# Lightning attention from the second group on in sub-chunks of 64: four products as 64x64 quarters

## The chip, the cores and the metric

The kernel runs on one core of a Trainium2 chip. TensorE multiplies (PE, with its weight loads as PEld), VectorE (DVE) and ScalarE (ACT) do the elementwise work, GpSimd (POOL) and SyncE (SP) mostly issue transfers. The metric is device time in microseconds (us) of one execution; the median of three runs of the kernel before is 673.94 us (673.93 to 674.11). A change of less than 0.2% can't be told from none.

## The reference

Inputs are q, k and v (4 batches, 8 heads, 768 positions, 64 dimensions), a decay per head, lam, and two weight matrices. First comes causal attention without a softmax, with a running state, in blocks of 64 positions:

```python
for b in range(nb):
    qb, kb, vb = (q[:, :, sl], k[:, :, sl], v[:, :, sl])
    intra = np.einsum('bhic,bhjc->bhij', qb, kb) * Dmask[None]      # lam ** (i - j), i >= j
    intra = np.einsum('bhij,bhjd->bhid', intra, vb)
    inter = np.einsum('bhid,bhde->bhie', qb * lam_pow[None], kv_state)
    out[:, :, sl] = intra + inter
    kb_dec = kb * rev_pow[None]
    kv_state = lam_block[None, :, None, None] * kv_state + np.einsum('bhsd,bhse->bhde', kb_dec, vb)
```

Its output, seen as x of 3072 tokens x 512, then goes through `h = x @ w_in` (512 x 2048), `g = h - tanh(h)` and `g @ w_out` (2048 x 512). The block length is free in exact arithmetic: any block length gives the same output.

## The kernel before, in words

The 768 positions are cut into six groups of 128 (`BLK`, `NG`); one group over four batches is 512 tokens. For each group the kernel does the attention, then the up product with w_in, the tanh step, and the down product with w_out. The two big products go by Strassen's scheme: seven products of sums of blocks in place of eight, and from the second group on some of the seven are split once more in the same way (`down_twice`, with the small products' results in the banks y and zw). The sums of blocks are made by VectorE: `sums_once`, `sums_twice`, and inside `down_twice` the step that subtracts s2 from a12, which the sixth of its seven products (x = 3) reads.

The attention of group g + 1 is computed in pieces between the up and down products of group g, a half (two batches) at a time. Its functions are these. `att_transpose` makes transposed q and k; from group 2 on VectorE transposes 32x32 blocks of specially loaded tiles (L306), and then makes qd, q times the powers of lam (L317). `att_scores` multiplies k and q (L327: 64 rows, 128 columns of weights, 128 moving columns, for each head) into the banks sp, and VectorE multiplies with the mask of decays (L331). `att_out` adds two products in the banks op: the inner product of state and qd (L375: 64x64 quarters, 128 columns) and the intra product of v and the masked scores (L381: 128 rows, 64 columns of weights, 128 columns). ScalarE copies the result to xt (L385). `att_state` multiplies k by its decay (L336), makes the product of k and v over the 128 positions (L349: 128 rows, 64 columns of weights, 64 moving columns) and updates the state (L354, L355). `att_sums` (L392 to L395) makes the Strassen sums of x once both halves are there.

Six places in the schedule take the attention of the next group: two in the last two steps of the up product (u = 2 and 3), one after each of the down products 2, 4, 5 and 6. Before, they take in this order: transposes of the first half; its scores; its output and state; transposes of the second half; its scores; its output, state and the sums. Group 1's attention is spread in the same six portions over group 0's plain down product. The order of instructions on each engine is not the program's alone: a scheduler moves whatever is not marked `keep_in_program_order` (`tied` in the code). Matrix banks in PSUM for the attention are four, shared in turn (tag "att").

A matmul of the program in float32 is two weight loads and two matmul records in the profile.

Of the kernel before, what the change touches and what calls it, by code (L numbers as in the profile page):

```python
# [9 lines left out]
F32 = mybir.dt.float32  # L10
# [3 lines left out]
AF = mybir.ActivationFunctionType  # L14
AL = mybir.AluOpType

BLK = 128
GB = 2
GRP = 512
CLAMP = 2.0 ** -15  # L20
# [3 lines left out]
def kernel(  # L24
# [32 lines left out]
    nc = tc.nc  # L57
    B, H, S, D = q.shape
    NTOK, DM = out.shape
    DFF = moe_w_in.shape[1]  # L60
    NP = H // 2
# [36 lines left out]
            nc.vector.tensor_tensor_scan(out=mask[:, j, p, :], data0=lam_all[:, h:h + 1].to_broadcast([128, BLK]),  # L98
                                         data1=ident, initial=0.0, op0=AL.mult, op1=AL.add)

    fwd = const.tile([128, NP, BLK], F32)

    def powers():
        for j in range(2):
            tc.keep_in_program_order(nc.vector.tensor_copy(
                fwd[ts(j, 64), :, 0], lam_all.rearrange("s (p j) -> s j p", j=2)[ts(j, 64), j, :]))
        m = 1
        while m < BLK:
            tc.keep_in_program_order(nc.vector.tensor_tensor(
                fwd[:, :, m:2 * m], fwd[:, :, 0:m], fwd[:, :, m - 1:m].to_broadcast([128, NP, m]), op=AL.mult))  # L110
            m *= 2
# [1 line left out]

    bwd = mask.rearrange("s j p i -> s p j i")[:, :, :, BLK - 1:BLK].to_broadcast([128, NP, 2, D])

    lam_blk = fwd[:, :, BLK - 1:BLK][:, None, :, :].to_broadcast([128, 2, NP, D])

    def tied(yes, op):
        return tc.keep_in_program_order(op) if yes else op
# [6 lines left out]
    def load_natural(g, b, names):  # L126
        for name, src, bufs in (("q", q, 2), ("k", k, 3), ("v", v, 4)):
            if name in names:
                x = (qpool if name == "q" else io).tile([128, H, D], F32, name=f"{name}_nat", tag=name, bufs=bufs)
                op = nc.sync.dma_start(out=x, in_=src[b, :, ts(g, BLK), :].rearrange("h s d -> s h d"))  # L130
                tc.keep_in_program_order(op)
                raw[g, b][name] = x

# [11 lines left out]
    def load(n):  # L145

        while at["loaded"] < min(n, len(chunks)):
            g, b = chunks[at["loaded"]]  # L150
            if g < GB:
                raw[g, b] = {}
                load_natural(g, b, "qkv")
                at["loaded"] += 1
                continue
            for b in range(B):
                raw[g, b] = {}
            nat = "kv" if g < NG - 1 else "v"

            first = (0, 1, 2) if g == GB else ()  # L160
            for b in first:
                load_natural(g, b, nat)
            for b in range(B - 1):
                load_blocks(g, b, "qk")
            load_blocks(g, 3, "q")
            for b in (0, 1):
                if b not in first:
                    load_natural(g, b, nat)
            load_blocks(g, 3, "k")
            for b in (2, 3):  # L170
                if b not in first:
                    load_natural(g, b, nat)
            at["loaded"] += B
# [99 lines left out]
    def bank(name, tag, bufs):  # L273
        return psum.tile([128, 512], F32, name=name, tag=tag, bufs=bufs)
# [23 lines left out]
    def att_transpose(g, bs):  # L298
        for b in bs:
            load(g * B + b + 1)  # L300
            t = raw[g, b]
            qt = work.tile([128, NP, BLK], F32, name="qt", tag="qt")
            kt = work.tile([128, NP, BLK], F32, name="kt", tag="kt")
            for dst, x in ((qt, "q"), (kt, "k")):
                if g >= GB:
                    tc.keep_in_program_order(nc.vector.transpose(out=dst.rearrange("d p i -> d (p i)"),  # L306
                                                                 in_=t[x + "b"].rearrange("d p r a -> d (p r a)")))
                else:
                    tp = bank("tp", "att", 4).rearrange("d (p s) -> d p s", p=NP)
                    for p in range(NP):  # L310
                        tied(g == 0 or p == 0, nc.tensor.transpose(out=tp[:, p, :], in_=t[x][:, 2 * p:2 * p + 2, :],
                                                                   identity=ident))
                    tied(g == 0, nc.scalar.activation(dst, tp, AF.Copy))
            qd = None
            if g > 0:
                qd = work.tile([128, NP, BLK], F32, name="qd", tag="qd")
                nc.vector.tensor_tensor(qd, qt, fwd, op=AL.mult)  # L317
            tr[g, b] = (qt, kt, qd)

    def att_scores(g, bs):  # L320
# [12 lines left out]

    def att_decay(g, b):
        kp = raw[g, b]["k"].rearrange("s (p j) d -> s p j d", j=2)
        tied(g != 1, nc.vector.tensor_tensor(kp, kp, bwd, op=AL.mult))  # L336

    def att_state(g, bs):
        if g == NG - 1:
            return  # L340

        kv = bank("kv", "att", 4).rearrange("d (b p e) -> d b p e", b=2, p=NP)
        for n, b in enumerate(bs):
            kd, vn = raw[g, b]["k"], raw[g, b]["v"]
            if g > 0:
                att_decay(g, b)
            for p in range(NP):
                for j in range(2):
                    tied(g == 0, nc.tensor.matmul(out=kv[ts(j, 64), n, p, :], lhsT=kd[:, 2 * p + j, :],  # L349
                                                  rhs=vn[:, 2 * p + j, :], start=n == 0 and p == 0, stop=True,  # L350
                                                  skip_group_check=True))
        st = state[:, bs[0]:bs[0] + 2]
        if g > 0:
            nc.vector.tensor_tensor(st, st, lam_blk, op=AL.mult)  # L354
            nc.vector.tensor_tensor(st, st, kv, op=AL.add)  # L355
        else:
            tied(True, nc.scalar.activation(st, kv, AF.Copy))

    def att_out(g, bs):
        half = bs[0] // 2  # L360
        xt[g, half] = xpool.tile([128, KI, HB], F32, name=f"xt{half}", tag=f"xt{half}")

        ops = [bank("op", "att", 4).rearrange("d (p b s) -> d p b s", p=2, b=2) for _ in range(2)]

        def dst(n, p, j):
            return ops[p // 2][ts(j if p < 2 else 1 - j, 64), p % 2, n, :]


        if g > 0:
            for n, b in enumerate(bs):  # L370
                for p in (0, 1):
                    for j in range(2):
                        r = ts(j, 64)
                        for pp in (p, p + 2):
                            nc.tensor.matmul(out=dst(n, pp, j), lhsT=state[r, b, pp, :], rhs=tr[g, b][2][r, pp, :],  # L375
                                             start=n == 0 and p == 0, stop=False, skip_group_check=True)
        for n, b in enumerate(bs):
            ss, vn = sc.pop((g, b)), raw[g, b]["v"]
            for p in range(NP):
                for j in range(2):  # L380
                    tied(g == 0, nc.tensor.matmul(out=dst(n, p, j), lhsT=vn[:, 2 * p + j, :], rhs=ss[:, j, p, :],  # L381
                                                  start=g == 0 and n == 0 and p % 2 == 0,
                                                  stop=n == 1 and p % 2 == 1, skip_group_check=True))
        for x in range(2):
            tied(g == 0, nc.scalar.activation(  # L385
                xt[g, half][:, 2 * x:2 * x + 2, :].rearrange("d p (b s) -> d p b s", b=2), ops[x], AF.Copy))

    def att_sums(g, bs):
        x0, x1 = xt[g, 0], xt[g, 1]
# [6 lines left out]
        xt[g] = dict(B11=b11, B21=b21, B22=b22, T1=tt[:, 0], T2=tt[:, 1], T3=b12, T4=tt[:, 2])  # L396

    def attention(g):
        pieces = [[(fn, g, bs) for fn in (att_transpose, att_scores, att_out, att_state)] for bs in ((0, 1), (2, 3))]
        pieces[1].append((att_sums, g, None))  # L400
        return pieces


    FACT = {1: ("A11", "B11"), 2: ("A12", "B21"), 3: ("S4", "B22"), 4: ("A22", "T4"), 5: ("S1", "T1"),
# [374 lines left out]
    def run(pieces):  # L779
        for fn, *args in pieces:  # L780
            fn(*args)
# [33 lines left out]
    for u in range(1, NU):  # L815
# [4 lines left out]
            load(2 * B)  # L820
        if u == 1:
            powers()
    p0, p1 = attention(1)
    weights(len(blocks) - 2 * (KH - 2))
    more = [p0[0:1], p0[1:2], p0[2:], p1[0:1], p1[1:2], p1[2:]]
    for kt in range(KH):
        down_plain(kt)
        sums_out(kt)
# [15 lines left out]
    up(1, 0, 1)  # L844
    for g in range(1, NG):
        last = g == NG - 1
        p0, p1 = attention(g + 1) if not last else ([], [])
        for u in range(NU):
            for n in (2, 6, 5, 7, 1, 4, 3) if g < GI else (1, 7, 3) if u == 0 else (6, 5, 1, 7, 3) if u + 1 < NU else (
                    6, 5, 7, 1, 3):  # L850
# [16 lines left out]
            if g == GI - 1:  # L867
                inner_weights(u)
            if not last and u > 1:
                run(p0[u - 2:u - 1])  # L870
        if twice(g, 4):
            sums_twice(g, 4)
        every(down(g, 2))
        run(p0[2:])
        sums_twice(g, 5)
        every(down_twice(g, 4, "z") if twice(g, 4) else down(g, 4))
        run(p1[0:1])
        sums_once(g, 21, 21, 11)
        sums_twice(g, 6)
        every(down_twice(g, 5, "w"))  # L880
        run(p1[1:2])
        if twice(g, 7):
            sums_twice(g, 7)
        every(down_twice(g, 6, "z"))
        if twice(g, 3):
            sums_twice(g, 3)
        run(p1[2:])
        every(down_twice(g, 7, "w") if twice(g, 7) else down(g, 7))
        if last:
            down_end(g)  # L890
# [45 lines left out]
```

## Time and profile before

| what | value |
|---|---|
| median of three runs | 673.94 us |
| span of the profiled execution, first to last instruction | 672.3 us |
| that execution's granted TensorE clock | 1.000 throughout |
| TensorE matmul busy | 661.7 us, 4824 records |
| VectorE busy | 481.3 us, 872 instructions |
| ScalarE busy | 194.8 us |
| GpSimd busy | 200.5 us |
| scores, L327 | 384 records, 25.2 us busy |
| intra product, L381 | 384 records, 23.6 us busy |
| state product, L349 | 320 records, 11.5 us busy |
| inner product, L375 | 320 records, 11.0 us busy |

The span lies 1.6 us below the median: the time also has what lies around the first and the last instruction. "Busy" of a group is the time in which at least one of its instructions ran; since matmuls overlap, the mean length of one record is far above the distance between their starts. What a product costs TensorE is read from the timeline, from its first start to the first start of what follows.

### The profile page before, as it was taken

Reading aid. Unit: us, or ns where it says so; the run is one execution under the profiler, and the core shown is the slowest. Engines: PE = TensorE matmul, PEld = TensorE weight load, DVE = VectorE, ACT = ScalarE, POOL = GpSimd, SP = SyncE. Lnnn points to the kernel's source line nnn. Section 1 sums busy time; section 2 is a strip of 40 time slices with the busy share of each in tenths; the row PEclk is TensorE's granted clock in tenths of the full one; section 3 lists DMA queues with packets and bytes.
Section 4 is the critical chain, followed back from the end, with each engine's and each line's share of the span. In section 5 each row is a group of like instructions: output and inputs, shape, how many; then the busy total and the mean of one; then the engine's idle time right before and its main releaser. Section 6 shows DMA issues by size and latency. Waiting matters only on the chain.

```text
span 672.3 us, 12869 instructions
## 1 busy us (share of the span) xinstructions
PE 661.7 (98%) x4824; PEld 576.3 (86%) x4824; DVE 481.3 (72%) x872; ACT 194.8 (29%) x373; POOL 200.5 (30%) x345
## 2 busy tenths in 40 slices
PE   8899999999999999999999999999999999999998
PEld 7688855558888999988999988899988899988997
DVE  4797867993887772499895379888358977357743
ACT  4564433423331111332112243112333112234110
POOL 0001424217332424244345201254300245400351
PEclk9999999999999999999999999999999999999999
DMA  9979799869855978587898632698730677610495
GB/s 209 222 205 236 238 268 255 290 147 271 249 148 139 243 191 210 127 239 236 228 285 253 176 80 58 150 292 255 225 73 13 160 236 220 217 35 1 126 289 164
DMA packets 162717, 128.80 MB, mean 192 GB/s; under 512 B 133856, under 2 KB 135008, under 8 KB 162656
## 3 DMA queue, kind: packets, MB, share of 16 engines
q0 software_dynamic: 28976, 96.49, 45.4%
q1 hardware_dynamic: 133536, 31.50, 23.6%
q8 instruction: 38, 0.62, 0.4%
q14 instruction: 23, 0.19, 0.1%
q10 hardware_dynamic: 144, 0.00, 0.0%
HBM read 103.55 MB, written 24.38 MB: 190 GB/s over the span
## 4 chain that ended last, share of the span: by engine, by line
PE 86%; issue 8%; DMA 2%; SPq 1%; POOL 1%; DVE 0%; ACT 0%; POOLq 0%; DVEq 0%; ACTq 0%
PE y L433 13%; PE y L695 11%; PE op L771 8%; PE z L433 8%; PE zw L695 8%; PE h L750 7%; PE w L642 4%; PE y L642 4%; PE y L517 4%; PE sp L327 3%; PE plain L642 3%; PE op L381 3%; PE z L517 2%; PE op L375 2%; PE kv L349 1%
## 5 line engine op out<-in xcount | busy, mean ns | idle before, releaser
L607 POOL DMA_DIRECT2D wb<-fine x147 | 79.4, 541 | 114.7 <-PE y L695 48.2
L610 POOL DMA_DIRECT2D wb<-factors x56 | 30.3, 543 | 155.2 <-PE y L642 97.3
L441 ACT ACTIVATE th<-g 128x512 f32<-128x512 f32 x76 | 47.6, 630 | 98.3 <-DVE g L446 33.2
L433 PE MATMUL y<-xt,w 128*128 128x256 f32 x320 | 74.0, 380 | 0.0
L433 PEld LDWEIGHTS y<-xt,w 128*128 128x128 f32 x320 | 59.9, 190 | 9.0 <-ACT g L521 0.9
L442 DVE TENSOR_TENSOR g<-g,th 128x512 f32<-128x512 f32 x76 | 51.9, 688 | 18.2 <-ACT th L441 18.1
L698 ACT ACTIVATE q<-y 128x128 f32<-128x128 f32 x84 | 23.3, 278 | 130.1 <-PE y L695 126.5
L750 PE MATMUL h<-xt,w 128*128 128x256 f32 x256 | 56.5, 381 | 2.0 <-DVE w L271 2.0
L771 PE MATMUL op<-wt,g 128*128 128x512 f32 x128 | 56.5, 595 | 0.0
L750 PEld LDWEIGHTS h<-xt,w 128*128 128x128 f32 x256 | 48.2, 190 | 9.2 <-DVE w L271 1.4
L695 PE MATMUL y<-wb,g 128*128 128x128 f32 x384 | 51.2, 278 | 0.0
L771 PEld LDWEIGHTS op<-wt,g 128*128 128x128 f32 x128 | 23.8, 190 | 27.7 <-issue 26.5
L695 PEld LDWEIGHTS y<-wb,g 128*128 128x128 f32 x384 | 46.4, 192 | 1.2 <-issue 0.3
L433 PE MATMUL z<-tt,ws 128*128 128x256 f32 x160 | 38.0, 380 | 0.0
L433 PE MATMUL z<-xt,ws 128*128 128x256 f32 x160 | 37.9, 380 | 0.0
L433 PE MATMUL y<-tt,ws 128*128 128x256 f32 x160 | 37.8, 379 | 0.0
L642 PE MATMUL y<-wb,g 128*128 128x256 f32 x160 | 35.6, 379 | 0.5 <-PE y L433 0.5
L198 POOL DMA_DIRECT2D raw<-in_moe_w_out_dram x16 | 8.9, 555 | 90.8 <-DVE g L758 52.3
L642 PE MATMUL w<-wb,g 128*128 128x256 f32 x160 | 35.8, 382 | 0.0
L331 DVE TENSOR_TENSOR ss<-sp,mask 128x512 f32<-128x512 f32 x48 | 30.9, 682 | 6.0 <-PE sp L327 6.0
L642 PEld LDWEIGHTS y<-wb,g 128*128 128x128 f32 x160 | 30.3, 190 | 5.0 <-PE y L433 0.9
L433 PEld LDWEIGHTS z<-xt,ws 128*128 128x128 f32 x160 | 30.3, 190 | 4.3 <-ACT g L449 0.2
(171 smaller groups left out, 1301.2 us busy)
## 6 DMA issues: line engine op xcount, KB each, us to landing
wb<-fine POOLq DMA_DIRECT2D x147, 256.0 KB, 3.9
wb<-factors POOLq DMA_DIRECT2D x68, 256.0 KB, 4.2
raw<-in_moe_w_out_dram POOLq DMA_DIRECT2D x16, 512.0 KB, 5.2
v_nat<-in_v_dram SPq DMA_DIRECT2D x24, 256.0 KB, 5.4
factors<-wt POOLq DMA_DIRECT2D x8, 768.0 KB, 5.0
wb<-fine_in POOLq DMA_DIRECT2D x24, 256.0 KB, 4.1
k_nat<-in_k_dram SPq DMA_DIRECT2D x20, 256.0 KB, 5.0
raw<-in_moe_w_in_dram SPq DMA_DIRECT2D x8, 512.0 KB, 5.9
```

The lines of the kernel that those rows point to most:

```text
L331: tied(g == 0, nc.vector.tensor_tensor(ss[:, j], sp[j], mask[:, j], op=AL.mult))
L433: nc.tensor.matmul(out=t[:, m, :], lhsT=wt[:, kt, ts(m, 128)], rhs=x[:, kt, :], start=first and m == 0 and kt == 0, stop=kt == 1, skip_gro ...
L441: nc.scalar.activation(th, src, AF.Tanh)
L442: nc.vector.tensor_tensor(dst(c), src, th, op=AL.subtract)
L517: nc.tensor.matmul(out=dst[:, ts(u, 128)], lhsT=a, rhs=b, start=x in (1, 2, 5) and u == 0, stop=True, skip_group_check=True)
L607: nc.gpsimd.dma_start(out=t.rearrange("p m c -> p (m c)"), in_=fine[TWICE.index(n_), SUB.index(x_)].rearrange("p u c -> p (u c)"))
L610: nc.gpsimd.dma_start(out=t, in_=factors[XAT[FACT[n_][1]]][:, 2 * x_:2 * x_ + 2, :])
L642: nc.tensor.matmul(out=t[:, m, :], lhsT=a[:, u, kt, ts(m, 128)], rhs=wb[:, kt, :], start=first and u == 0 and m == 0 and kt == 0, stop=u = ...
L695: nc.tensor.matmul(out=dst, lhsT=a[:, u, :], rhs=wb[:, ts(u, 128)], start=x in (1, 2) and u == 0, stop=u == NU - 1, skip_group_check=True)
L698: nc.scalar.activation(keep, dst, AF.Copy)
L750: tied(u == 0, nc.tensor.matmul(out=hm[c][:, m, :], lhsT=w1[u][:, i, a, ts(m, 128)], rhs=xt[0, t][:, i, :], start=m == 0 and i == 0, stop= ...
L771: nc.tensor.matmul(out=obank[b], lhsT=g, rhs=wt[:, 2 * a:2 * a + 2, :], start=kt == 0 and a == 0, stop=kt == KH - 1 and a == 1)
```

## The change

From group 1 on, a group of 128 positions is handled as two sub-chunks of 64. The scores are made within each sub-chunk only, as four 64x64 quarters with 64 moving columns (sub-chunk x, head parity j), so the block of scores between the second and the first sub-chunk is no longer made. What the second sub-chunk gets from the first goes through a middle state: `sub_state` makes a state product for each sub-chunk, and the middle state md, that is state times lam^64 plus the first product. `sub_inter` multiplies q of the first sub-chunk by the state and q of the second by md. `sub_carry` makes the new state from md and the second product. Group 0 keeps the old form.

The powers of lam and the mask for the decay go to 64 instead of 128, and a copy puts the mask's lower quarter to the front. The mask products of a half are two instructions with both batches in place of four. The last group now makes the state product of its first sub-chunk (before, it made none), so it also loads k for those 64 positions. `intra` is called twice for a half: in `sub_inter` for the first sub-chunk of the even heads and the second of the odd ones, and, one place later, in `sub_intra` for the others. A one-column read by ScalarE (`seen`) follows `sub_inter`.

The six places now take: transposes of the first half; its scores and state product; its inner product with half the intra product, carry, and the transposes of the second half; the rest of the intra product, then scores and state product of the second half; its inner product and carry; the rest of the intra product and the sums.

```diff
+SUBL = 64
...
-    fwd = const.tile([128, NP, BLK], F32)
+    fwd = const.tile([128, NP, SUBL], F32)
+    mask_sub = mask[:, :, :, 0:SUBL]
...
+        nc.vector.tensor_copy(mask_sub[ts(1, 64)], mask[ts(1, 64), :, :, ts(1, SUBL)])
...
+                n = SUBL if name == "k" and g == NG - 1 else BLK
...
-                nc.vector.tensor_tensor(qd, qt, fwd, op=AL.mult)
+                nc.vector.tensor_tensor(qd.rearrange("d p (x i) -> d p x i", x=2),
+                                        qt.rearrange("d p (x i) -> d p x i", x=2),
+                                        fwd[:, :, None, :].to_broadcast([128, NP, 2, SUBL]), op=AL.mult)
...
+    def sub_scores(g, bs):
+
+        sp = [bank("sp", "att", 4).rearrange("s (b p i) -> s b p i", b=2, p=NP) for _ in range(2)]
+        for n, b in enumerate(bs):
+            qt, kt, _ = tr[g, b]
+            for p in range(NP):
+                for x in range(2):
+                    for j in range(2):
+                        r, c = ts(j, 64), ts(x, SUBL)
+                        nc.tensor.matmul(out=sp[j][c, n, p, :], lhsT=kt[r, p, c], rhs=qt[r, p, c],
+                                         start=n == 0 and p == 0, stop=n == 1 and p == NP - 1, skip_group_check=True)
+        ss = work.tile([128, 2, 2, NP, SUBL], F32, name="ss", tag="ss")
+        for j in range(2):
+            nc.vector.tensor_tensor(ss[:, j], sp[j],
+                                    mask_sub[:, j][:, None, :, :].to_broadcast([128, 2, NP, SUBL]), op=AL.mult)
+        sc[g, bs] = ss
+
+    def sub_state(g, bs):
+
+        subs = range(1 if g == NG - 1 else 2)
+        kv = [bank("kv", "att", 4).rearrange("d (b p e) -> d b p e", b=2, p=NP) for _ in subs]
+        for b in bs:
+            att_decay(g, b)
+        for n, b in enumerate(bs):
+            kd, vn = raw[g, b]["k"], raw[g, b]["v"]
+            for p in range(NP):
+                for x in subs:
+                    for j in range(2):
+                        h, r = 2 * p + j, ts(x, SUBL)
+                        nc.tensor.matmul(out=kv[x][ts(j, 64), n, p, :], lhsT=kd[r, h, :], rhs=vn[r, h, :],
+                                         start=n == 0 and p == 0, stop=n == 1 and p == NP - 1, skip_group_check=True)
+        st, md = state[:, bs[0]:bs[0] + 2], work.tile([128, 2, NP, D], F32, name="mid", tag="mid", bufs=1)
+        nc.vector.tensor_tensor(md, st, lam_blk, op=AL.mult)
+        nc.vector.tensor_tensor(md, md, kv[0], op=AL.add)
+        kvs[g, bs] = kv, md
...
+        for x in range(2):
+            for n, b in enumerate(bs):
+                qd = tr[g, b][2]
+                for p in (0, 1):
+                    for pp in (p, p + 2):
+                        for j in range(2):
+                            r = ts(j, 64)
+                            tied(True, nc.tensor.matmul(
+                                out=out_part(g, n, x, pp, j), lhsT=md[r, n, pp, :] if x else state[r, b, pp, :],
+                                rhs=qd[r, pp, ts(x, SUBL)], start=x == 0 and n == 0 and p == 0, stop=False,
+                                skip_group_check=True))
+        intra(g, bs, 0)
+
+        nc.scalar.activation(seen, obanks[g][1][:, 0, 0, 0:1], AF.Copy)
+
+    def intra(g, bs, other):
+        ss = sc[g, bs]
+        for n, b in enumerate(bs):
+            vn = raw[g, b]["v"]
+            for p in (0, 1):
+                for pp in (p + 2, p) if other else (p, p + 2):
+                    for j in range(2):
+                        x = j ^ other
+                        r = ts(x, SUBL)
+                        tied(True, nc.tensor.matmul(
+                            out=out_part(g, n, x, pp, j), lhsT=vn[r, 2 * pp + j, :], rhs=ss[r, j, n, pp, :],
+                            start=False, stop=other == 1 and n == 1 and p == 1, skip_group_check=True))
...
+    def sub_carry(g, bs):
+
+        kv, md = kvs.pop((g, bs))
+        if g < NG - 1:
+            st = state[:, bs[0]:bs[0] + 2]
+            nc.vector.tensor_tensor(st, md, lam_blk, op=AL.mult)
+            nc.vector.tensor_tensor(st, st, kv[1], op=AL.add)
...
-        pieces = [[(fn, g, bs) for fn in (att_transpose, att_scores, att_out, att_state)] for bs in ((0, 1), (2, 3))]
-        pieces[1].append((att_sums, g, None))
-        return pieces
+        (t0, s0, k0, i0, c0, o0), (t1, s1, k1, i1, c1, o1) = (
+            [(fn, g, bs) for fn in (att_transpose, sub_scores, sub_state, sub_inter, sub_carry, sub_intra)]
+            for bs in ((0, 1), (2, 3)))
+        return [[t0], [s0, k0], [i0, c0, t1], [o0, s1, k1], [i1, c1], [o1, (att_sums, g, None)]]
```

In the changed file the lines stand lower: scores L393, mask L397, decay L346, state product L413, middle state L416 and L417, inner product L438, intra product L455, carry L472 and L473, sums of x L479 to L482, small down products L783, the step that the sixth of them reads L788, and their results L793 to L799.

More of the change, by code (lines that the diff above doesn't have):

```diff
@@ L106, in powers @@
                 fwd[ts(j, 64), :, 0], lam_all.rearrange("s (p j) -> s j p", j=2)[ts(j, 64), j, :]))
+        nc.vector.tensor_copy(mask_sub[ts(1, 64)], mask[ts(1, 64), :, :, ts(1, SUBL)])
         m = 1
-        while m < BLK:
+        while m < SUBL:
             tc.keep_in_program_order(nc.vector.tensor_tensor(
@@ L114 @@
     bwd = mask.rearrange("s j p i -> s p j i")[:, :, :, BLK - 1:BLK].to_broadcast([128, NP, 2, D])
-    lam_blk = fwd[:, :, BLK - 1:BLK][:, None, :, :].to_broadcast([128, 2, NP, D])
+    bwd_sub = mask_sub.rearrange("s j p i -> s p j i")[:, :, :, SUBL - 1:SUBL].to_broadcast([128, NP, 2, D])
+    lam_blk = fwd[:, :, SUBL - 1:SUBL][:, None, :, :].to_broadcast([128, 2, NP, D])
     def tied(yes, op):
@@ L129, in load_natural @@
                 x = (qpool if name == "q" else io).tile([128, H, D], F32, name=f"{name}_nat", tag=name, bufs=bufs)
-                op = nc.sync.dma_start(out=x, in_=src[b, :, ts(g, BLK), :].rearrange("h s d -> s h d"))
+                n = SUBL if name == "k" and g == NG - 1 else BLK
+                op = nc.sync.dma_start(out=x[0:n],
+                                       in_=src[b, :, g * BLK:g * BLK + n, :].rearrange("h s d -> s h d"))
                 tc.keep_in_program_order(op)
@@ L157, in load @@
                 raw[g, b] = {}
-            nat = "kv" if g < NG - 1 else "v"
+            nat = "kv"
             first = (0, 1, 2) if g == GB else ()
@@ L335, in att_decay @@
         kp = raw[g, b]["k"].rearrange("s (p j) d -> s p j d", j=2)
-        tied(g != 1, nc.vector.tensor_tensor(kp, kp, bwd, op=AL.mult))
+        n, by = (SUBL if g == NG - 1 else BLK), bwd if g == 0 else bwd_sub
+        tied(g != 1, nc.vector.tensor_tensor(kp[0:n], kp[0:n], by[0:n], op=AL.mult))
     def att_state(g, bs):
-        if g == NG - 1:
-            return
         kv = bank("kv", "att", 4).rearrange("d (b p e) -> d b p e", b=2, p=NP)
@@ L344, in att_state @@
             kd, vn = raw[g, b]["k"], raw[g, b]["v"]
-            if g > 0:
-                att_decay(g, b)
             for p in range(NP):
                 for j in range(2):
[L349 to L357, printed above, removed]
+                    tied(True, nc.tensor.matmul(out=kv[ts(j, 64), n, p, :], lhsT=kd[:, 2 * p + j, :],
+                                                rhs=vn[:, 2 * p + j, :], start=n == 0 and p == 0, stop=True,
+                                                skip_group_check=True))
+        tied(True, nc.scalar.activation(state[:, bs[0]:bs[0] + 2], kv, AF.Copy))
     def att_out(g, bs):
@@ L366, in dst @@
             return ops[p // 2][ts(j if p < 2 else 1 - j, 64), p % 2, n, :]
[L369 to L376, printed above, removed]
         for n, b in enumerate(bs):
@@ L380, in att_out @@
                 for j in range(2):
-                    tied(g == 0, nc.tensor.matmul(out=dst(n, p, j), lhsT=vn[:, 2 * p + j, :], rhs=ss[:, j, p, :],
-                                                  start=g == 0 and n == 0 and p % 2 == 0,
-                                                  stop=n == 1 and p % 2 == 1, skip_group_check=True))
+                    tied(True, nc.tensor.matmul(out=dst(n, p, j), lhsT=vn[:, 2 * p + j, :], rhs=ss[:, j, p, :],
+                                                start=n == 0 and p % 2 == 0, stop=n == 1 and p % 2 == 1,
+                                                skip_group_check=True))
@@ L384, in att_out @@
         for x in range(2):
-            tied(g == 0, nc.scalar.activation(
+            tied(True, nc.scalar.activation(
                 xt[g, half][:, 2 * x:2 * x + 2, :].rearrange("d p (b s) -> d p b s", b=2), ops[x], AF.Copy))
+    kvs = {}
+    seen = const.tile([128, 1], F32)
+    def sub_scores(g, bs):
[13 more added lines that the diff above has]
+        sc[g, bs] = ss
@@ new lines, with out_part, sub_inter @@
+    obanks = {}
+    def out_part(g, n, x, p, j):
+        return obanks[g][p // 2][ts(j if p < 2 else 1 - j, 64), p % 2, n, ts(x, SUBL)]
+    def sub_inter(g, bs):
+        half = bs[0] // 2
+        xt[g, half] = xpool.tile([128, KI, HB], F32, name=f"xt{half}", tag=f"xt{half}")
+        obanks[g] = [bank("op", "att", 4).rearrange("d (p b s) -> d p b s", p=2, b=2) for _ in range(2)]
+        md = kvs[g, bs][1]
+        for x in range(2):
[8 more added lines that the diff above has]
+                                rhs=qd[r, pp, ts(x, SUBL)], start=x == 0 and n == 0 and p == 0, stop=False,
+                                skip_group_check=True))
+        intra(g, bs, 0)
+        nc.scalar.activation(seen, obanks[g][1][:, 0, 0, 0:1], AF.Copy)
@@ new lines, in sub_intra @@
+    def sub_intra(g, bs):
+        half = bs[0] // 2
+        intra(g, bs, 1)
+        for x in range(2):
+            nc.scalar.activation(xt[g, half][:, 2 * x:2 * x + 2, :].rearrange("d p (b s) -> d p b s", b=2),
+                                 obanks[g][x], AF.Copy)
+    def sub_carry(g, bs):
[4 more added lines that the diff above has]
+            nc.vector.tensor_tensor(st, st, kv[1], op=AL.add)
@@ L822 @@
             powers()
-    p0, p1 = attention(1)
+    more = attention(1)
     weights(len(blocks) - 2 * (KH - 2))
-    more = [p0[0:1], p0[1:2], p0[2:], p1[0:1], p1[1:2], p1[2:]]
     for kt in range(KH):
@@ L846 @@
         last = g == NG - 1
-        p0, p1 = attention(g + 1) if not last else ([], [])
+        att = attention(g + 1) if not last else [[]] * 6
         for u in range(NU):
@@ L869 @@
             if not last and u > 1:
-                run(p0[u - 2:u - 1])
+                run(att[u - 2])
         if twice(g, 4):
@@ L873 @@
         every(down(g, 2))
-        run(p0[2:])
+        run(att[2])
         sums_twice(g, 5)
         every(down_twice(g, 4, "z") if twice(g, 4) else down(g, 4))
-        run(p1[0:1])
+        run(att[3])
         sums_once(g, 21, 21, 11)
@@ L880 @@
         every(down_twice(g, 5, "w"))
-        run(p1[1:2])
+        run(att[4])
         if twice(g, 7):
@@ L886 @@
             sums_twice(g, 3)
-        run(p1[2:])
+        run(att[5])
         every(down_twice(g, 7, "w") if twice(g, 7) else down(g, 7))
```

## The prediction

> **What bounds the kernel now.** I read the busy shares on the page first, then the chain that ended last, then the groups of attention instructions, and last the timelines of TensorE and VectorE through one half of the attention.
>
> ```profile
> PE 661.7 (98%) x4824; PEld 576.3 (86%) x4824; DVE 481.3 (72%) x872; ACT 194.8 (29%) x373; POOL 200.5 (30%) x345
> PE 86%; issue 8%; DMA 2%; SPq 1%; POOL 1%; DVE 0%; ACT 0%; POOLq 0%; DVEq 0%; ACTq 0%
> ```
>
> TensorE is busy for 98% of the span and is nearly the whole chain; nothing else is waited for long. So the time is TensorE's work plus its waits, and a change is worth what it takes out of either. VectorE's 72% is an average, and its own timeline has to be read where the change is.
>
> The groups by line (busy time, mean of one, idle before) give the four attention products:
>
> ```profile
> L327 PE MATMUL sp<-qt,kt 64*128 64x128 f32 x384 | 25.2, 279 | 1.4 <-ACT kt L313 1.4
> L381 PE MATMUL op<-ss,v_nat 128*64 128x128 f32 x384 | 23.6, 276 | 0.0
> L349 PE MATMUL kv<-v_nat,k_nat 128*64 128x64 f32 x320 | 11.5, 223 | 0.3 <-DMA v_nat<-in_v_dram 0.2
> L375 PE MATMUL op<-qd,state 64*64 64x128 f32 x320 | 11.0, 275 | 0.0
> ```
>
> One matmul of the program is two records. The means are latencies of overlapping records; the cost is the pace. Each appearance of a product is 32 records. TensorE's timeline for the first half of group 3 (start, length, line):
>
> ```profile
> 314.05 1.89 PE L433 MATMUL z<-xt,ws 128*128 128x256 f32 x8
> 315.87 2.06 PE L327 MATMUL sp<-qt,kt 64*128 64x128 f32 x32
> 317.85 7.17 PE L642 MATMUL w<-wb,g 128*128 128x256 f32 x32
> 324.96 1.10 PE L375 MATMUL op<-qd,state 64*64 64x128 f32 x32
> 325.99 1.97 PE L381 MATMUL op<-ss,v_nat 128*64 128x128 f32 x32
> 327.79 1.10 PE L349 MATMUL kv<-v_nat,k_nat 128*64 128x64 f32 x32
> 328.82 1.16 PE L695 MATMUL y<-wb,g 128*128 128x128 f32 x8
> ...
> 333.39 1.06 PE L695 MATMUL zw<-wb,g 128*128 128x128 f32 x8
> ```
>
> From start to next start, scores take 1.99 us, inner (state) products 1.03, intra products 1.80, state products 1.03: 5.85 for a half. VectorE in the same stretch:
>
> ```profile
> 314.47 0.68 DVE L679 TENSOR_TENSOR s<-g 128x512 f32<-128x512 f32 x1
> ...
> 316.28 0.68 DVE L469 TENSOR_TENSOR g<-g,z 128x512 f32<-128x512 f32 x1
> ...
> 318.08 0.68 DVE L442 TENSOR_TENSOR g<-g,th 128x512 f32<-128x512 f32 x1
> ...
> 322.88 1.28 DVE L336 TENSOR_TENSOR k_nat<-k_nat,mask 128x512 f32<-128x512 f32 x2
> ...
> 329.50 0.68 DVE L355 TENSOR_TENSOR state<-state,kv 128x512 f32<-128x512 f32 x1
> 330.91 0.69 DVE L700 TENSOR_TENSOR g<-g,s 128x512 f32<-128x512 f32 x1 [0.73 <-PE zw L695]
> ```
>
> From 314.47 to 330 an operation starts every 0.602 us without a gap: here VectorE has no spare time, though TensorE does not yet wait for it. That is where a shorter or reordered TensorE stretch can run into it.
>
> **TensorE's part.** Before, ten halves at 5.85, less 2 x 1.03 (the last group has no state product), plus 0.65 for four products that took longer (2.11, 1.90, 1.90 and 1.17) make 57.1 us. Around each stretch of attention the large matmuls lose a little: the eight z records, 0.216 apart, would end 1.73 after 314.05, and sp starts after 1.82 (0.1 late); 32 w records would take 6.91 and take 7.11, 0.1 on each side. With 20 stretches x 0.2: 61.1 us in all.
>
> The change makes 32 program matmuls, 64 records, of each product in a half: 10 x 256 = 2560 records, less 64 because the last group needs only the first sub-chunk's state: 2496. Their pace is not in the trace. The state product, also 64 columns, shows 29.2 ns per record with two tiles side by side (pairs 58.5 apart). The inner product already uses 64x64 quarters, with 128 columns: 27.3 per record, in groups of four 109 apart whose four starts are 7 ns apart. So four quarters do run at once, and columns set the time: 58.5/4 = 14.6 ns is what I take, as the rows with the same columns and the same quarters agree on it. The lower end is half the inner product's, 13.7; the upper end is 29.2, no gain from fewer columns. Issue does not forbid 14.6: after a wait that ended at 245.67 the queue took 32 TensorE instructions in 0.13 us, 4.1 ns each, and 14.6 per record is 7.3 per instruction (a weight load and a matmul). In the last group 64 state records have only two tiles: 29.2. Together 2432 x 14.6 + 64 x 29.2 = 37.4 us.
>
> A switch costs: beyond the pace, sp's stretch spends 0.15 and inner, intra and state together 0.30 inside, 0.15 for a stretch of one kind, and 0.2 around it: 0.35. The order in which the scheduler lays out the changed kernel has 34 stretches (5 in group 1, 8 in group 2, 7 in each later one): 11.9 us; 0.2 to 0.5 each are the ends (7 to 17). After: 49.3, so TensorE alone gains **11.8 us** (662.1).
>
> [...]
>
> **VectorE's part.** Counts hardly move: 20 more state operations, 4 more decays (half the partitions in the last group), 20 fewer mask products (two per half with both batches in one), one power fewer, one copy more: +4, 2.4 us beside TensorE. ScalarE gets ten one-column reads, with 29% of its time used. SP gets four more loads (k of the last group, 64 rows), in a queue whose earlier loads landed 5 us after issue and that are needed tens of us later. Hidden by idle engines; bounds 0 and about 0.5 us each should one come late.
>
> The order does move. The state products go ahead of the inner ones, up to 7 us earlier, and with them the decays and the middle state; the second half's transposes go ahead of the first twice-split down product instead of behind it. I lay the changed kernel's VectorE order over the times above, at 0.602 each.
>
> - *First half, groups 3 and 4.* From 314.47 the operation that prepares the sixth of the seven small products (L788, before L700) is the 32nd; 31 x 0.602, plus 0.2 for a tanh result that ends at 317.68, starts it at 333.3 and ends it at 334.0. Before it stand the decays, middle state, carry (2), four transposes and two scaled q. TensorE would be there at 333.39 - 6.25 (before's 5.85 + 0.4) + 4.32 (224 records x 14.6, three stretches) = 331.46 and gets on at 334.1: **2.6 us** of waits, some 0.9 of them at the state product: its second batch could start at 321.1 (scores from 315.87, 0.94 and 0.25 long, 16 w records, half a state product), and the decay it reads, the twelfth operation, ends at 322.0.
> - *The block behind the second half.* Before, 3.9 us of attention lay between two blocks, now one stretch of 0.8. VectorE has five operations on the earlier block's results (L793 to L799), four sums of x (0.6 each) and only then L788, which ends 5.7 us after that block; the sixth product wants it after 0.82 + 5 x 0.89 = 5.3: **0.5 us**.
> - *Group 5*: no carry, two operations less: 2.6 - 1.2 + 0.5 = **1.9**.
> - *Group 2*: from the scores at 207.84 it is 1.19 + 20 w records (4.32) + 0.1 to the state product, 213.45, and 213.9 for its second batch; the decay for that, behind ten short operations on weights (0.2 each), ends at 215.3: **1.4**.
> - *Group 1*: intra, scores and state stand in one stretch, and the state banks wait for two ScalarE copies of 0.6: **0.5**.
>
> The second half's carries, decays and middle states come out ahead of their readers by 0.2 us or more. Here are the operations moved forward, as they run before, behind the block:
>
> ```profile
> 335.35 0.70 DVE L306 STREAM_TRANSPOSE qt<-q_blk 128x512 f32<-128x512 f32 x1
> 335.98 0.67 DVE L306 STREAM_TRANSPOSE kt<-k_blk 128x512 f32<-128x512 f32 x1
> 336.57 0.65 DVE L317 TENSOR_TENSOR qd<-qt,fwd 128x512 f32<-128x512 f32 x1
> ```
>
> Their data are there: the last of these loads is issued at 319.2, 5.7 us to landing, and the transposes would start at 329.8.
>
> New waits: 2 x (2.6 + 0.5) + 1.9 + 1.4 + 0.5 = 10.0 us. The ends: 0, if the order leaves VectorE slack that I do not see; 18, if its step is nearer the 0.69 that one operation lasts (then 31 operations end 2.7 us later in each of three groups).
>
> **Sum.** 11.8 - 10.0 = 1.8 us gained. The profiled execution's span is 672.3, 1.6 below the median of 673.94; I take that difference as unchanged and forecast 672.1, at the edge of what can be told from no change (0.2%, 1.35 us).
>
> **Rivals.**
> 1. *The waits do not come* (VectorE finds gaps, or the state product's wait replaces the later one wholly): 662 to 667. For it: TensorE's small products wait nowhere for VectorE now. Against: sixteen us without one gap in VectorE.
> 2. *Slower, by VectorE alone*: the sixth product of the block behind the first half waits for the transposes and the carry longer than 2.6 us. Starts up to 0.73 apart occur on VectorE (331.80 to 332.53), and the carry's second operation needs its first. At 0.69 a step the waits are 18 us: 680. It decides from 0.6 us more in each of groups 3 to 5.
> 3. *The quarters do not pack*: at 27.3 per record (inner product) 68.3 + 11.9 = 80.2 against 61.1, 19 us slower, 693, with VectorE then in time. Break-even without waits is (61.1 - 11.9 - 1.9)/2432 = 19.5 ns. For it: no row with 64 columns in quarters. Against: four starts 7 ns apart.
>
> **Chances.** The sum's case 0.55 (its own range 667 to 677: faster 0.30, same 0.12, slower 0.13), rival 1 0.18, rival 2 0.17, rival 3 0.10. Faster 0.48, same 0.12, slower 0.40. The range 662 to 681 leaves out rival 3 and the outermost of the others.
>
> **What would show it.** Right: about 14.6 ns per record at L393, L413, L438, L455, with 2496 records in all; TensorE idle ahead of L413 (released by the decay L346) and ahead of the zw of L783 (released by L788) in groups 3 to 5, together near 10 us; VectorE still without a gap there. [...]

## The result: 0.76% slower, and the profile after

The changed kernel takes 679.15 us (678.42 to 679.70, four runs) against 673.93 us: a ratio of 1.0076, with a 95% interval from 1.0061 to 1.0090. The forecast was 672.1 and leaned to faster. The time lies inside the stated range and on the other side.

The page's busy shares and its chain, after:

```profile
PE 653.7 (96%) x6104; PEld 564.2 (83%) x6104; DVE 483.8 (71%) x876; ACT 196.1 (29%) x383; POOL 199.0 (29%) x345
PE 77%; DVE 11%; DMA 4%; SPq 3%; issue 2%; ACT 1%; POOL 1%; DVEq 0%; ACTq 0%; POOLq 0%
```

TensorE is busy for 8 us less, in a span (677.6) that is 5.3 us longer. Before, the chain was 86% TensorE and no VectorE to speak of; now VectorE has 11% of it. So the work did get shorter, and TensorE now stands and waits. The waits of TensorE, in the view that sums them by what ended them (us in total, times, longest; "issue" means that the profile names nothing that ended the wait):

```profile
PE zw L783 <- DVE g L788: 4.1, 6, 1.6
PE kv L413 <- DVE k_nat L346: 3.0, 5, 0.8
PE tp L318 <- ACT qt L320: 2.7, 1, 2.7
...
PE y L730 <- DMA wb<-factors: 2.0, 2, 1.4
PE z L521 <- DVE g L552: 1.8, 1, 1.8
...
PE sp L393 <- issue: 1.2, 1, 1.2
PE op L859 <- issue: 0.5, 1, 0.5
```

Two of these seven lines were forecast, the first and the second. The others were not. The quarters themselves, in the groups by line:

```profile
L455 PE MATMUL op<-ss,v_nat 64*64 64x64 f32 x640 | 13.4, 221 | 0.0
L413 PE MATMUL kv<-v_nat,k_nat 64*64 64x64 f32 x576 | 12.5, 222 | 3.4 <-DVE k_nat L346 3.0 <-ACT xt L464 0.4
L393 PE MATMUL sp<-qt,kt 64*64 64x64 f32 x640 | 11.8, 220 | 1.2 <-issue 1.2
L438 PE MATMUL op<-qd,state 64*64 64x64 f32 x320 | 6.9, 224 | 0.0
L438 PE MATMUL op<-qd,mid 64*64 64x64 f32 x320 | 6.5, 218 | 0.0
```

These are 2496 records, as counted beforehand. Single records start in fours 7 ns apart, one four every 58.5 ns: 14.6 ns per record, where the range went from 13.7 to 29.2. TensorE's timeline through the first half of group 3, the place for which the waits were worked out (a bracket at a row's end gives the idle time before it and what ended it):

```profile
319.31 1.16 PE L393 MATMUL sp<-qt,kt 64*64 64x64 f32 x64
320.40 3.72 PE L730 MATMUL w<-wb,g 128*128 128x256 f32 x16
324.61 1.30 PE L413 MATMUL kv<-v_nat,k_nat 64*64 64x64 f32 x64 [0.49 <-DVE k_nat L346]
325.84 3.72 PE L730 MATMUL w<-wb,g 128*128 128x256 f32 x16
329.49 0.69 PE L438 MATMUL op<-qd,state 64*64 64x64 f32 x32
...
334.72 1.06 PE L783 MATMUL y<-wb,g 128*128 128x128 f32 x8
337.33 1.16 PE L783 MATMUL zw<-wb,g 128*128 128x128 f32 x8 [1.55 <-DVE g L788]
```

And VectorE ahead of that last product:

```profile
331.69 0.68 DVE L472 TENSOR_TENSOR state<-mid,fwd 128x512 f32<-128x512 f32 x1
332.41 0.69 DVE L473 TENSOR_TENSOR state<-state,kv 128x512 f32<-128x512 f32 x1
333.01 0.70 DVE L313 STREAM_TRANSPOSE qt<-q_blk 128x512 f32<-128x512 f32 x1
...
336.02 0.65 DVE L324 TENSOR_TENSOR qd<-qt,fwd 128x512 f32<-128x512 f32 x1
336.59 0.68 DVE L788 TENSOR_TENSOR g<-g,s 128x512 f32<-128x512 f32 x1
```

Carry, transposes and scaled q stand in front of L788 without a gap, as laid out beforehand, and a product that would have started at 335.6 starts at 337.33.

To add the losses up I take, between two starts on TensorE, the distance less the pace of that kind of record: what a wait costs, which is a little more than the idle time that the profile gives. Against the forecast's own terms:

| term | forecast, us | measured, us |
|---|---|---|
| attention on TensorE, with its switches (61.1 before) | 49.3 | 50.1 |
| state products waiting for decays, groups 2 to 5 | 4.1 | 3.8 |
| sixth small product of the first block, groups 3 to 5 | 3.9 | 3.8 |
| the block behind the second half, groups 3 to 5 | 1.5 | 1.3 |
| group 1, state banks | 0.5 | 0.85 |
| group 1, transposes waiting for ScalarE (L318) | 0 | 2.85 |
| z waiting for L552, at 179 us | 0 | 1.94 |
| no releaser named (sp at 446, op at 124) | 0 | 2.1 |
| y waiting for loads of wb, at 304 and 313 (0.7 before) | 0 | 1.6 more |
| waits of before that are smaller or gone | 0 | -2.1 |

The first five rows come to 0.6 us more than the forecast (0.8 more in the first, 0.2 less in the other four); the last five make 6.4. 672.1 + 0.6 + 6.4 = 679.1.

### The profile page after: what moved, and what is told of

It reads as the page before. It is cut to its first block, busy times and chain, and to the rows that moved or that the text cites. A ratio compares the mean times of both kernels' runs of the same rounds, so it can differ in the third digit from the quotient of the medians.

```text
span 677.6 us, 15460 instructions
## 1 busy us (share of the span) xinstructions
PE 653.7 (96%) x6104; PEld 564.2 (83%) x6104; DVE 483.8 (71%) x876; ACT 196.1 (29%) x383; POOL 199.0 (29%) x345
## 4 chain that ended last, share of the span: by engine, by line
PE 77%; DVE 11%; DMA 4%; SPq 3%; issue 2%; ACT 1%; POOL 1%; DVEq 0%; ACTq 0%; POOLq 0%
PE y L521 13%; PE y L783 9%; PE z L521 8%; PE op L859 8%; PE h L838 7%; PE zw L783 7%; PE y L730 5%; PE y L605 4%; PE plain L730 3%; PE z L605 2%; PE w L730 1%; SPq L149 1%; PE kv L413 1%; DVE g L530 1%; PE w L605 1%
## 5 line engine op out<-in xcount | busy, mean ns | idle before, releaser
L783 PE MATMUL y<-wb,g 128*128 128x128 f32 x384 | 51.1, 278 | 0.0
L783 PEld LDWEIGHTS y<-wb,g 128*128 128x128 f32 x384 | 46.4, 192 | 0.7
L783 PE MATMUL zw<-wb,g 128*128 128x128 f32 x256 | 34.4, 277 | 4.1 <-DVE g L788 4.1
L730 PE MATMUL y<-wb,g 128*128 128x256 f32 x160 | 35.9, 380 | 2.0 <-DMA wb<-factors 2.0
L730 PE MATMUL w<-wb,g 128*128 128x256 f32 x160 | 36.8, 384 | 0.0
L730 PEld LDWEIGHTS y<-wb,g 128*128 128x128 f32 x160 | 30.2, 190 | 6.8 <-issue 1.8
L783 PEld LDWEIGHTS zw<-wb,g 128*128 128x128 f32 x256 | 31.1, 192 | 5.3 <-DVE g L788 5.3
```

What stands on the lines that cost most here:

```text
L730: nc.tensor.matmul(out=t[:, m, :], lhsT=a[:, u, kt, ts(m, 128)], rhs=wb[:, kt, :], start=first and u == 0 and m == 0 and kt == 0, stop=u = ...
L783: nc.tensor.matmul(out=dst, lhsT=a[:, u, :], rhs=wb[:, ts(u, 128)], start=x in (1, 2) and u == 0, stop=u == NU - 1, skip_group_check=True)
```

## The experiments

My theory was now: the quarters gain about 11 us, and most of the 16 us of new waits come from the places at which the pieces are put, in separate and curable ways: VectorE's queue ahead of L788, the decays, and, in group 1, ScalarE's queue. The rival: quarters cost this by themselves, through instructions and transfers, wherever they stand. All edits are to the changed kernel; times are medians with those of the kernel before on the same chip beside them.

### Group 1's transposes one place later

```diff
+        if g == 1:
+            return [[t0], [s0, k0], [i0, c0], [o0, t1], [s1, k1], [i1, c1, o1, (att_sums, g, None)]]
         return [[t0], [s0, k0], [i0, c0, t1], [o0, s1, k1], [i1, c1], [o1, (att_sums, g, None)]]
```

> Only group 1's places change: its second half's transposes go one place later, behind the rest of the first half's intra product, its scores and state product another place later, and its last three steps come together. Theory (order): TensorE stood 2.85 us at these transposes, because the copies that free their banks are queued on ScalarE behind the weights' rounding, and what VectorE and GpSimd lost there comes back as the 1.94 us ahead of z at L521; both go, 679.1 becomes about 674.4. Rival (transfers): the 1.94 is a crowded memory system's own and stays, 676.3. Rival (no effect): the wait moves to another product of group 1, 679.

Measured: 674.72 us beside 673.68, ratio 1.0016 (1.0004 to 1.0027), 4.4 us below the change. The wait at the transposes falls from 2.85 to 0.3, that of z from 1.94 to 0.9. The rows of the changed kernel show what stood there (TensorE, then ScalarE):

```profile
107.72 1.02 PE L859 MATMUL op<-wt,g 128*128 128x512 f32 x2
111.43 0.65 PE L318 MATMUL tp<-ident,k_nat 128*128 128x128 f32 x4 [2.69 <-ACT qt L320]
```

```profile
110.15 0.68 ACT L271 ACTIVATE r<-raw 128x512 int32<-128x512 uint32 x1 [3.10 <-DVE wt L278]
110.73 0.17 ACT L444 ACTIVATE seen<-op 128x1 f32<-128x1 f32 x1
110.78 0.60 ACT L320 ACTIVATE qt<-tp 128x512 f32<-128x512 f32 x1
```

In group 1 the transposes are TensorE's, and ScalarE copies them. The copy stands behind a rounding step of the weights (L271) that has itself waited 3.1 us for VectorE. TensorE needs the copy to have a bank for the next transpose. So ScalarE, busy for 29% of the span, held TensorE up by order alone. The 1.94 ahead of z goes with it at least in part: half of it went. There VectorE stood 2.42 us for a transfer (fine<-wt, ahead of L678), with L552, which z needs, next in its queue.

### The same edit in groups 2 to 5

```diff
+        if g > 1:
+            return [[t0], [s0, k0], [i0, c0], [o0, t1], [s1, k1], [i1, c1, o1, (att_sums, g, None)]]
         return [[t0], [s0, k0], [i0, c0, t1], [o0, s1, k1], [i1, c1], [o1, (att_sums, g, None)]]
```

> Same edit in groups 2 to 5 only. Theory (VectorE's queue): the sixth small product of the first block waits for L788 because carry and transposes stand ahead of it (1.71, 1.71, 0.40 us), and the fourth block's waits 0.43 three times; with the transposes behind that block and more attention between the last blocks all of this goes, 5.1 us, 679.1 becomes about 674.0. Rival: VectorE has no time anywhere in this stretch and the wait moves to the second half's state product, whose decays now come right behind its masks: 677 to 679.

Measured: 675.26 us beside 673.68, ratio 1.0021 (1.0007 to 1.0035), 3.9 us below the change. TensorE's waits, the top of the view:

```profile
PE kv L413 <- DVE k_nat L346: 3.0, 5, 0.8
PE tp L318 <- ACT qt L320: 2.7, 2, 2.0
```

No wait for the step ahead of the sixth product is left, in any block, and the wait for the decays is the same 3.0 to the tenth. The second half's state product, whose decays now come right behind its masks, doesn't wait. The theory holds, the rival falls, though the gain is 3.9 us where the waits that went were forecast to give 5.1. In seven of the twelve executions the mean granted clock was 0.992 to 0.997, which may be the rest; in the profiled one it was 1.000.

### The decays one place earlier

```diff
+    def decays(g, bs):
+        for b in bs:
+            att_decay(g, b)
...
-        for b in bs:
-            att_decay(g, b)
+        if bs[0] == 2:
+            decays(g, bs)
...
-        return [[t0], [s0, k0], [i0, c0, t1], [o0, s1, k1], [i1, c1], [o1, (att_sums, g, None)]]
+        return [[t0, (decays, g, (0, 1))], [s0, k0], [i0, c0, t1], [o0, s1, k1], [i1, c1], [o1, (att_sums, g, None)]]
```

> The first half's decays are made one place earlier, with its transposes. Theory (the decays alone): TensorE's waits at L413 (0.92 and 0.72 in group 2, 0.65, 0.77 and 0.77 in groups 3 to 5) go, 3.8 us: 675.3. Rival (a full queue): in groups 3 to 5 VectorE runs without a gap, so an earlier decay makes nothing after it earlier; TensorE comes to the sixth small product sooner and waits there 0.7 longer in each; only group 2's 1.6 are gained: 677.5.

Measured: 679.0 us beside 673.68, ratio 1.0086 (1.0060 to 1.0112): nothing gained. The waits at the state products are gone, all five. Those at the sixth product grew from 1.71, 1.71 and 0.40 to 2.52, 2.20 and 1.48, which is what the rival said, with 0.5 to 1.1 each for its 0.7. One row, where lines stand four lower:

```profile
338.35 0.82 PE L787 MATMUL zw<-wb,g 128*128 128x128 f32 x5 [2.36 <-DVE g L792]
```

By these waits 1.4 us should have been gained, and weren't. After the longer waits TensorE's clock fell. The table by stretch, whose columns are the stretch, its length, TensorE's busy time and records, the granted clock, and the transfers' share and rate:

```profile
330.00:338.00 8.00, 5.99 (x132) 1.00 1.08 296
338.00:343.00 5.00, 4.65 (x92) 0.66 0.83 213
343.00:350.00 7.00, 7.00 (x147) 1.00 0.61 145
```

The 0.66 is a mean. With the stretch cut where the clock changes, it is half speed for 3.4 us:

```profile
339.26:342.66 3.40, 3.40 (x63) 0.50 0.70 172
```

That costs 1.7 us. The same 3.4 us at 0.50 begin at 113.97, 182.24 and 445.07, each behind a wait of 2.2 us or more, so this execution lost some 6.8 us to the clock, more than the 1.4. It is the longest of the six, 682.21 us at a mean clock of 0.990; the shortest took 676.99 us at 0.997. In the changed kernel the waits of 1.7 us are followed by a clock of 1.00.

### The quarters in the old places

```diff
-        return [[t0], [s0, k0], [i0, c0, t1], [o0, s1, k1], [i1, c1], [o1, (att_sums, g, None)]]
+        return [[t0], [s0], [k0, i0, c0, o0], [t1], [s1], [k1, i1, c1, o1, (att_sums, g, None)]]
```

> The quarters alone, in the places of the kernel before: transposes; scores; state product, inner, carry and whole intra product together; the same for the second half. Theory (it is the order that costs): TensorE's gain of 10.9 us stays, the waits at L318, L413 and L788 go, and instead each half waits for the middle state, some 0.5 to 0.8 us in ten halves: 668 to 671, faster than before. Rival (quarters cost it by themselves, through instruction supply or transfers): 676 or more.

Measured: 687.72 us beside 673.68, ratio 1.0209 (1.0179 to 1.0238). My expectation fails by 17 us at least, and the rival's number is met for another reason: without a named releaser TensorE lost 0.2 us. One line of the waits holds the cause, and two of the timeline show it:

```profile
PE op L438 <- DVE mid L417: 17.1, 10, 2.6
```

```profile
331.82 1.16 PE L413 MATMUL kv<-v_nat,k_nat 64*64 64x64 f32 x64
332.80 0.65 PE L438 MATMUL op<-qd,state 64*64 64x64 f32 x32
335.83 0.69 PE L438 MATMUL op<-qd,mid 64*64 64x64 f32 x32 [2.38 <-DVE mid L417]
```

The second sub-chunk's inner product reads the middle state, which VectorE makes from the state product just ended, and not at once but in its turn in a full queue: 1.7 us on the mean, not the 0.5 to 0.8 I had allowed for the operation and its signal. Here too the clock falls behind long waits: to 0.50 for 6.8 us from 224.05, and for 3.4 us from 142.13, 336.69, 445.92 and 551.73, the last behind a wait of 1.8 us. At half speed these 20.5 us cost up to 10 more in the profiled execution, which is the longest of the six (690.57 us). So the change's earlier place for the state product is worth far more than the 3.8 us that it costs at the decays. The sub-chunks bring a chain from TensorE to VectorE and back that the kernel before did not have.

### Both edits, all groups

```diff
-        return [[t0], [s0, k0], [i0, c0, t1], [o0, s1, k1], [i1, c1], [o1, (att_sums, g, None)]]
+        return [[t0], [s0, k0], [i0, c0], [o0, t1], [s1, k1], [i1, c1, o1, (att_sums, g, None)]]
```

> The later place for the second half's transposes in all groups, 1 to 5, the decays as in the change. Theory (order, two separate losses): the gains of the two earlier runs, 4.4 in group 1 (674.7 against 679.1) and 3.9 in groups 2 to 5 (675.3), add up: 670.8, faster than before, with the waits at L413 (about 3 us) still there. Rival (a common limit that both only share in): 674 to 675.

Measured: 669.12 us beside 673.57, ratio 0.9941 (0.9921 to 0.9961): faster than the kernel before. The two gains add (8.3 expected, 10.0 measured), and the waits at L413 are still 3.0. The 1.94 ahead of z is gone altogether, which half of it was not with group 1 alone.

### Both edits and the earlier decays

The two edits above together.

> As late_t1, and the first half's decays one place earlier as well. Theory (full queue): the earlier decays gained nothing because VectorE had the transposes in front of L788 and ran full up to it; with these behind the block there is room, so the 3.8 us at L413 now go and do not come back at L788: 667. Rival: the queue is as full without them, and the waits move to L788 or to the middle state again: 670 to 671.

Measured: 664.38 us beside 673.57, ratio 0.9866 (0.9846 to 0.9886). The earlier decays, worth nothing by themselves, are worth 4.7 us here. The scheduler also sets the first half's state product right behind its scores, a switch less in four groups. Lines stand four lower; the same stretch of group 3:

```profile
313.94 1.16 PE L393 MATMUL sp<-qt,kt 64*64 64x64 f32 x64
314.93 1.11 PE L417 MATMUL kv<-v_nat,k_nat 64*64 64x64 f32 x64
315.97 7.17 PE L734 MATMUL w<-wb,g 128*128 128x256 f32 x32
323.07 0.69 PE L442 MATMUL op<-qd,state 64*64 64x64 f32 x32
...
328.31 1.06 PE L787 MATMUL y<-wb,g 128*128 128x128 f32 x8
329.20 1.06 PE L787 MATMUL zw<-wb,g 128*128 128x128 f32 x8
```

No bracket stands behind any of them: the state product, the middle state and the sixth small product all come without a wait. This is a version that beats both kernels, by 1.3% and 2.2%.

### Four times the scores

```diff
-        for n, b in enumerate(bs):
+        for n, b in [(n, b) for _ in range(4) for n, b in enumerate(bs)]:
```

> The changed kernel with each half's score products made four times over, 128 program matmuls in a row instead of 32: the cost of a long run of quarters by itself. Theory (quarters at 14.6 ns): each half's scores last 0.94 x 4 = 3.75 us, 28 us more in ten halves, less what other waits then hide. Rival (instruction supply): 512 instructions in a row at 7.3 ns each outrun what is fetched, and TensorE stands without a releaser, as for 1.44 us in one half of the changed kernel: 1 us or more in most halves, 5 us or more in all.

Measured: one run of 745.27 us. The scores' group, and one half's timeline:

```profile
L393 PE MATMUL sp<-qt,kt 64*64 64x64 f32 x2560 | 44.7, 225 | 25.9 <-issue 25.9
```

```profile
376.91 1.93 PE L393 MATMUL sp<-qt,kt 64*64 64x64 f32 x120
380.61 2.09 PE L393 MATMUL sp<-qt,kt 64*64 64x64 f32 x128 [1.77 <-issue]
384.34 0.34 PE L393 MATMUL sp<-qt,kt 64*64 64x64 f32 x8 [1.63 <-issue]
```

From start to next start the ten halves' scores take 69.5 us, not 37.5. Each run of 512 instructions stands at least once, for 1.4 to 3.6 us, waiting for nothing that the profile names, after 120 to 198 records. The clock, 0.50 for 23.9 us in all, slowed this execution as well. In this half the two halts lie 128 records apart, that is 256 instructions. By an estimate that is a packet of q8, a queue whose kind the page calls "instruction": this run's page gives it 1.03 MB in 63 packets, 16 KB each, and over TensorE's 2 x 8024 instructions 64 bytes for one (before, 0.62 MB over 2 x 4824, the same). The times of these packets in the trace fit: each of the twelve halts ends 1.3 to 1.6 us after the end of a q8 packet (here the packets end at 379.21 and 382.87, the halts at 380.61 and 384.34). The rival's halts came: from 376.91 to 384.34, 248 records take 7.43 us, 15 ns per instruction, where quarters at 14.6 ns need one every 7.3. In the changed kernel the like are the 1.44 at 446 and, by the same label, the 0.64 at 124; both end 1.5 us after a q8 packet (446.13 and 123.77). Its scores come in runs of 64 records, and one run of ten stands. That the halt is the fetch of instructions is inferred from this spacing and these times; no row names it.

### One quarter at a time

```diff
-        for n, b in enumerate(bs):
-            qt, kt, _ = tr[g, b]
-            for p in range(NP):
-                for x in range(2):
-                    for j in range(2):
+        for x in range(2):
+            for j in range(2):
+                for n, b in enumerate(bs):
+                    qt, kt, _ = tr[g, b]
+                    for p in range(NP):
                         r, c = ts(j, 64), ts(x, SUBL)
```

> The changed kernel with the score products in another order: all eight of one quarter, then all eight of the next, in place of the four quarters in turn. Theory (neighbours in the order must use different quarters to run side by side): each record takes the 58.5 ns of 64 columns, 64 records 3.7 us in place of 1.0, some 27 us more in ten halves, less what waits of VectorE then hide (about 5). Rival (TensorE finds work for the other quarters further on in its queue of some 30 instructions): below 2.5 us for a half's scores.

Measured: one run of 691.05 us. The scores' group, and a half of them:

```profile
L393 PE MATMUL sp<-qt,kt 64*64 64x64 f32 x640 | 33.8, 221 | 0.0
```

```profile
323.26 3.40 PE L393 MATMUL sp<-qt,kt 64*64 64x64 f32 x64
326.59 1.78 PE L730 MATMUL w<-wb,g 128*128 128x256 f32 x7
```

64 records take 3.33 us where they took 1.09: 52 ns each. The same products, on the same quarters, cost three times as much when neighbours in the order share a quarter. The kernel loses 11.9 us and not 27, because the scores' 22 us hide waits of VectorE, as expected, and the halts without a releaser.

## Why the prediction was wrong

**What bounds the kernel: right, as far as it went.** TensorE, and then VectorE in the stretch without a gap. All waits that I worked out beforehand, nearly all of them from VectorE's order, came, in their places, 9.8 us for 10.0, and the two late-transposes runs and the earlier decays show the causes of all but group 1's 0.85 one by one.

**TensorE's part: right.** 50.1 us for 49.3; the pace that I took is the measured one to the nanosecond. Rival 3 falls, and "one quarter at a time" shows what its case would have been. With neighbours on different quarters the starts lie 7 ns apart in a four and 14.6 ns apart on the mean at 64 columns (L393 from 319.31 on).

**"Issue does not forbid 14.6": wrong.** I read 4.1 ns per instruction off a burst of 32 and needed 7.3. The burst was no measure of a longer run: in "four times the scores" 248 records in a row took 15 ns per instruction, halts included. That the burst came out of a reserve is my reading; no run shows it. If both halts of the changed kernel without a releaser are of this kind, they cost 2.1 us.

**"Group 1: 0.5": the step that failed most.** I priced the state banks and left out that the transposes, which I had followed on VectorE in groups 2 to 5, are TensorE's and ScalarE's in group 1, and moved there too. What they were moved past on ScalarE is a rounding step that waits for VectorE. This term measured 2.85, and 1.94 at z follows group 1's order as well: 4.4 us went with the one edit. The five profiled executions with the change's order in group 1 lose 1.6 to 2.2 us at z, the three with the later transposes 0.9 at most.

**Loads.** I set those of k and q at nothing, as landing long before need, and they did. The loads of wb ahead of L730, which my sum doesn't have, came 1.6 us later in sum. GpSimd issues them, and its rows before and after (the changed kernel's stand second) show it held up by a transfer:

```profile
295.53 0.76 POOL L601 DMA_DIRECT2D wb<-factors  x1 [1.40 <-DMA fine<-wb]
300.24 0.76 POOL L689 DMA_DIRECT2D wb<-factors  x1 [4.37 <-DMA fine<-wb]
```

This wait of GpSimd is 1.4 to 1.8 us in the kernel before and the three longest-running versions, which lose 0.7 at y, as before. It is 3.3 to 4.7 in the changed kernel and the five other edits, which lose 0.4 to 2.3 us more there; the fastest has the 4.70 and loses 3.0. Why the transfer takes longer in these, and whether the change has a part in it, stays open.

**The sum.** The gain and the waits that I saw cancelled to 1.8 us, so 6.4 us of waits I did not see decided the sign. Rival 2, the slower one, got its direction and nearly its time (680) and not its mechanism: VectorE's step stayed 0.60. That its time was so near is luck.

## What to carry to other kernels

When a piece is moved in a schedule, follow it on every engine that runs any of it, stage by stage: the same function can run on other engines in the first group than in the rest. Making a saturated engine's work shorter is worth what the next engine's queue has room for (here 11.0 us shorter, with 9.8 us of new waits, nearly all for VectorE); a wait removed in a full queue comes back behind it, and the same edit pays once the queue has room (the earlier decays: nothing alone, 4.7 us with the later transposes). Price a new round trip between two engines by the length of the queue on the far one (in the old places 1.7 us on the mean), not by the operation (0.5 to 0.8 with its signal, as I had it).

## What the runs showed of the hardware that I had not expected

- In "four times the scores" TensorE, at 14.6 ns per record, first stands after 120 to 198 records, for 1.4 to 3.6 us, and goes on 1.3 to 1.6 us after the end of a q8 packet. In the changed kernel, with large matmuls in between, TensorE stood twice without a releaser, for 1.44 and 0.64 us.
- With the earlier decays four waits of TensorE of 2.2 us or more were each followed by 3.4 us at a granted clock of 0.50, which costs 1.7 us more; in the old places the clock fell to 0.50 five times, once for 6.8 us. The length of the wait alone does not decide it: the clock fell behind 1.8 us in the old places, but not there behind two of 1.9, nor behind 2.85 in the changed kernel's group 1; behind the changed kernel's waits of 1.7 it stayed at 1.00. With the earlier decays the falls begin at 113.97, 182.24, 339.26 and 445.07, which is 20, 46 and 31 times 3.413 us from one to the next, so where a wait lies may count too.
- The order of matmuls alone makes a factor of three: a half's 64 score records of 64 columns take 3.33 us (52 ns each) with neighbours on one quarter, and 1.09 us, at 14.6 ns from start to start, with neighbours on four.
